# Block-sparse attention with a gated feed-forward, one core: other places for copies, turns, squares, tables and group entries

## The chip, the core and the metric

The kernel runs on one core of one Trainium2 chip. The core has a matrix engine (PE; PEld is its weight load), VectorE (DVE), ScalarE (ACT), GpSimd (POOL), a queue engine (SP), and 16 DMA engines. Each engine executes its own instructions strictly in the order in which the program issues them, and waits on semaphores for the others. The metric is the time of one execution in microseconds, the median of several runs.

## The reference, cut to what matters

```python
# q, k, v: (4 batches, 8 heads, 768, 64); blocks of 32, 24 blocks a sequence
scores = (q @ k.T) / sqrt(64)
# a query block sees: itself and one block either side, blocks 0 and 23, and three sampled blocks;
# query blocks 0 and 23 see everything
attn = softmax(where(mask, scores, -1e9)) @ v
x = attn with the heads side by side            # (3072, 512)
xn = x / sqrt(mean(x*x) + 1e-6) * rms_g
out = (silu(xn @ w_gate) * (xn @ w_val)) @ w_out   # 512 -> 1536 -> 512, float32
```

## The kernel before

**Passage.** Batch 0 is computed densely with a mask, in three groups of 256 queries (`groups`), each looping over the 8 heads `h`. A head makes two score parts (L527, three matmuls each, exponentials on ACT, L530) and, one head later, the product with the values (`late_pv` -> `pv`, L536, then reciprocal and scaling into `stage` on DVE, L545 and L546). At four points of each head `position()` takes pieces of the feed-forward of the group before out of the list `fill`; `small_work(gi, h)` follows each of these points. During the last group (`gi == 2`) the keys and queries of batch 1 are turned (`turn_first` -> `turn`, six PE transposes into a bank `tqk`, L455, and one copy into `KT1` or `QN1`, L457), the indices are worked out (`indices`, L385 to L410), the table of values is written (`table`, L446), and the first sparse chunk's keys (`gather_k`, `sampled_k`: L471, L476, L485), values (`gather_v`, L512) and queries (`gather_q`: `Qd`, L500) are collected. The queries' copies wait in `first_queries`, ScalarE's copies of sampled keys in `first_keys`. `after_pv` puts the squares of the group (`part_squares`, L570) into `later` or runs them; `dense_power` on POOL (L577), `dense_scale` (L585) and `dense_turn` (L596, L600) follow.

**Banks.** A matmul writes into one of eight PSUM banks. In the passage `bank()` gives out three of them in turn (the ring), for gate, value, down, turned and other tiles; one more ("ot", from `ps_o`) holds the product with the values and some turns; four are the score buffers. After the passage `bank()` goes round all eight. So a bank is free for the third (later the eighth) request after its own, once its reader is done.

**Feed-forward.** A group's pieces are, for twelve blocks `f` in turn, `gate(f)` (L732; tanh on ACT, L736) and `val(f)` (L743; on DVE `u`, L747, frees the gate's bank, and `hps`, L751, frees the value's bank), then four `down` parts (L761) a chunk, each of which needs three of the `hps`. `enter` sets the rate: the pieces in the list over the positions up to the next entry.

**Sparse steps.** Batches 1 to 3 are 18 chunks of 128 queries, six a batch, in six groups of 2, 3, 4, 4, 3, 2 chunks. Step `i` has ten positions `n`; `do(n, f)` lists a job at position `n`, and after a position's jobs one `position()` follows. Step `i` multiplies chunk `i-1` with its values (`values`, L644, at 0 and 1), normalises it (`normalise`, L669 and L670, at 1 and 2), squares it on ACT at 4, takes the power on POOL at 5 (L681, L682), scales and turns it at 7 (`x_turned`: `xs` on DVE, L694, and a transposing DMA of SP's queue into `xg`, L696); it makes chunk `i`'s scores from position 1 on (L620), and collects chunk `i+1` (`nx`): the window of the keys on DVE (`gk[0]`, 1536 columns), for the first two chunks of a batch also the edge keys (`gk[1:]`), sampled keys on POOL and ACT, the queries (`gq`, four copies, eight for the chunk of edge blocks), and the values by POOL's indirect DMA (two for `nx` at 1 and 2, two for `nx+1` at 6 and 7). One batch's keys, queries and table are made ready during the batch before.

Of the kernel before, what the change touches and what calls it, by code (L numbers as in the profile page):

```python
# [18 lines left out]
def kernel(  # L19
# [425 lines left out]
    def table(b):  # L445
        nc.gpsimd.dma_start(out=vtab[b][0:NT, :].rearrange("(p c) x -> p (c x)", c=HC),  # L446
                            in_=Vs[b % 2].rearrange("p c h x -> p (c h x)"))
# [60 lines left out]
    def gather_v(i, js=range(QB)):  # L508
        b, qbs = chunks[i]
        for j in js:  # L510
            if qbs[j] not in (0, NB - 1):
                nc.gpsimd.indirect_dma_start(  # L512
                    vgs[i % 3][:, j, :], None, vtab[b][:],
                    bass.IndirectOffsetOnAxis(ap=vidx[:, qbs[j]:qbs[j] + 1], axis=0))
# [52 lines left out]
    def part_squares(e, it, lo, hi):  # L567
        junk = work.tile([P, DM], BF16, name="junk", tag="junk", bufs=1)
        part = e["stage"][:, it, lo:hi]
        nc.vector.tensor_tensor_reduce(  # L570
            out=junk[:, 0:hi - lo], in0=part, in1=part, scale=1.0,
            scalar=(e["ssq"][:, it:it + 1] if lo else DM * 1e-6),
            op0=ALU.mult, op1=ALU.add, accum_out=e["ssq"][:, it:it + 1])
# [229 lines left out]
    NPD = 4 * H  # L803

    def after_pv(e, h):
        if h == H - 3:
            later.append(lambda: part_squares(e, 1, 0, (H - 2) * D))
        if h == H - 2:
            later.append(lambda: part_squares(e, 0, 0, (H - 1) * D))
        if h == H - 1:  # L810
            for it in range(2):
                part_squares(e, it, (H - 2 if it else H - 1) * D, H * D)
            dense_power(e)

    def late_pv():
# [24 lines left out]
    def indices(n):  # L840
        for _ in range(n):
            if index:
                index.pop(0)()
# [55 lines left out]
    def small_work(gi, h):  # L899
        if gi == 1 and h > 3 or gi == 2 and h < 4:  # L900
            next_address()
        if first_keys:
            first_keys.pop(0)()

    def turn_first(gi, h):
        if gi == 1 and h in (0, 2, 4):
            transpose_qk(h // 2 + 1, 1, 1, HC, h == 0, (dve, dve))
        if gi == 2:
            for pr, which, copy, spare in {
                    1: ((0, 0, act, False), (0, 1, dve, True)),  # L910
                    2: ((1, 0, act, True), (1, 1, dve, True)), 3: ((2, 0, act, True),),
                    4: ((2, 1, dve, True), (3, 0, act, True)), 5: ((3, 1, dve, True),)}.get(h, ()):
                turn(1, pr, which, copy, spare)
            if h == 5:
                first_queries.extend(gather_q(0, dve))
# [82 lines left out]
    for gi, grp in enumerate(groups):  # L998
        if gi == 0:
            continue  # L1000
        cur = begin(grp)
        for h in range(H):
            ex = ex_tile()
            thin = gi == 1 and h < TX
            dense_scores(grp, h, 0, ex)
            if h == 1 and ending is not None:
                dense_scale(ending, 1)
            if h == TX and ending is not None:
                dense_turn(ending, 0)
                if gi == 1:  # L1010
                    dense_turn(ending, 1)
                    enter_dense(ending, NPD + 4)
                    ending = None
            if thin and h > 0:
                keep_busy(1, 512)
            position()
            small_work(gi, h)
            if gi == 1 and h == 0:
                late_pv()
                last = late_pv()  # L1020
            dense_scores(grp, h, 1, ex)
            side_work(gi, h)
            position()
            small_work(gi, h)
            if thin:
                keep_busy(1, 512)
            if gi > 1 or h > 0:
                last = late_pv()
            if gi == 2:
                indices(5)  # L1030
            for _ in range(2 if first_queries else 0):
                first_queries.pop(0)()
            if last is not None:
                ending = last
            position()
            small_work(gi, h)
            position()
            small_work(gi, h)
            while later:
                later.pop(0)()  # L1040
            if h == TX and ending is not None:
                dense_turn(ending, 1)
                enter_dense(ending, NPD - 4 * TX - 4 + 10)
                ending = None
            turn_first(gi, h)
            if h == 0 and ending is not None:
                dense_scale(ending, 0)
            waiting.append((cur, h, ex))
# [8 lines left out]
    NPOS = 10  # L1057
    entry = {}
    for g, m in enumerate(sgroups[:-1]):
        entry[(min(m[-1] + 2, NCH), 3)] = g  # L1060

    def distance(i, n):

# [9 lines left out]
    for i in range(NCH + 1):  # L1073
        jobs = {}

        def do(n, f):
            jobs.setdefault(n, []).append(f)

        b, s = divmod(i, PB)
        b += 1  # L1080
        nx = i + 1 if i + 1 < NCH else None
        if i == 0:
            do(0, late_pv)
            do(3, lambda: dense_scale(cur, 0))
            do(3, lambda: dense_scale(cur, 1))
            do(5, lambda: dense_turn(cur, 0))
            do(6, lambda: dense_turn(cur, 1))
            do(6, lambda: enter_dense(cur, distance(0, 6)))
            do(4, lambda: nc.vector.memset(Qd[1], 0.0))
            do(3, lambda: load_kq(2, 3))  # L1090
            do(7, lambda: gather_v(1, (2, 3)))
        else:
            do(0, lambda: values(i - 1, 0))
            do(1, lambda: normalise(i - 1, 0))
            do(1, lambda: values(i - 1, 1))
            do(2, lambda: normalise(i - 1, 1))
            do(4, lambda: squares(i - 1))
            do(5, lambda: rms_power(i - 1))
            do(8 if i - 1 in sgroups[-1] else 7, lambda: x_turned(i - 1))
        if i < NCH:  # L1100
            n = bursts(i)
            for part in range(n):
                do(1 + part, lambda part=part: scores(i, part))
        if b + 1 < B and s <= NP:
            if s < NP:
                do(9 if s == 0 else 0, lambda: cast_v(b + 1, s, act))
            if s > 0:
                do(6, lambda: turn(b + 1, s - 1, 0, act, True))
                do(9, lambda: turn(b + 1, s - 1, 1, act, True))
            if s == 0 and b == 1:  # L1110
                do(8, lambda: nc.vector.memset(Vs[0][:, :, :, D:VW], 1.0))
            if s == NP - 1:
                do(2, lambda: table(b + 1))
        if nx is not None:
            at = 6 if nx == 1 else 0
            gk, gq = list(gather_k(nx, dve)), list(gather_q(nx, dve))
            do(at, gk[0])
            for m, x in enumerate(gk[1:]):
                do(min(at + 1, 8) + m, x)
            for m, x in enumerate(gq):  # L1120
                do(at + (3 if at == 0 else 1) + m * 4 // len(gq) * (at == 0) + m // 2 * (at > 0), x)
            kact, kpool = sampled_k(nx, "act"), sampled_k(nx, "pool")
            for x in kpool:
                do(at, x)
            for m, x in enumerate(kact):
                do(at + (m + 1) * (NPOS - 1 - at) // len(kact), x)
            if nx > 1:
                do(1, lambda: gather_v(nx, (2,)))
                do(2, lambda: gather_v(nx, (3,)))
            if nx + 1 < NCH:  # L1130
                do(6, lambda: gather_v(nx + 1, (0,)))
                do(7, lambda: gather_v(nx + 1, (1,)))
        for m in range(min(6, len(by_need)) if i < 2 else 0):
            do(m, next_address)

        bl, sl = divmod(i + 2, PB)
        if 0 < bl and bl + 2 < B and sl < NP:
            do(9, lambda: load_kq(bl + 2, sl))
        bv, sv = divmod(i + 3, PB)
        if 0 < bv and bv + 2 < B and sv < NP:  # L1140
            do(7, lambda: load_v(bv + 2, sv))
        for n in range(NPOS):
            if (i, n) in entry:
                g = entry[(i, n)]
                enter(ffn_pieces(xgs[g], sizes[g], chunk_store(sgroups[g])), distance(i, n))
            for x in jobs.get(n, ()):
                x()
            position()
# [35 lines left out]
```

## Time and profile before

| | |
|---|---|
| median of 3 runs (range) | 296.19 us (296.06 to 297.59) |
| the profiled execution: its own time, span | 295.37 us, 293.6 us |
| granted clock of PE | 0.998 |
| PE busy | 277.5 us (95%) |
| DVE, ACT, POOL busy | 216.4, 197.6, 151.5 us |
| passage with batch 1's turns (the last dense group) | from 44 to 77 us |
| first, second, third feed-forward group of sparse chunks enter at | 105.9, 133.8, 168.5 us |

A line of the timeline reads: start and duration in us, engine, line, operation, out<-in, count, and in brackets how long the engine had stood idle just before and what ended that. Seven instructions merged into one line are written x7. Since matmuls overlap, the next matmul may start before the one in the line has ended.

### The profile page before, as it was taken

The numbers are of one execution on the slowest core, as the hardware profiler recorded it, in microseconds if no ns is written. First come the engines' busy times: TensorE is split into PE (matmuls) and PEld (weight loads), VectorE is DVE, ScalarE is ACT, GpSimd is POOL, SyncE is SP. The second block draws the span as 40 slices with busy tenths as digits, with TensorE's granted clock in tenths as the row PEclk, the third lists the DMA queues.
The fourth block names the chain that finished last, engine by engine and source line by source line (L and its number), as shares of the span: only waits on it lengthen the run. The fifth ranks groups of instructions, "written<-read, shape, count | busy, mean of one in ns | idle before, by whom it ended". The sixth has DMA issues, their size and how long they took to land.

```text
span 293.6 us, 9868 instructions
## 1 busy us (share of the span) xinstructions
PE 277.5 (95%) x3863; PEld 184.2 (63%) x3863; DVE 216.4 (74%) x596; ACT 197.6 (67%) x466; POOL 151.5 (52%) x247
## 2 busy tenths in 40 slices
PE   8898999897899999699989999999999999899995
PEld 6686885776577678565655555545545456555783
DVE  7888887778889949966998479885399931784480
ACT  4996785677488888669999777577747484522431
POOL 9948135669587653885888463637641710001000
PEclk9999999999999999999999999999999999999999
DMA  7999999997986488997997933517740523000102
GB/s 134 297 215 201 208 206 281 301 262 216 175 238 165 131 279 154 163 239 237 227 190 198 311 107 99 145 44 201 232 120 2 138 78 82 36 2 36 74 1 71
DMA packets 38514, 47.70 MB, mean 162 GB/s; under 512 B 12272, under 2 KB 30468, under 8 KB 38468
## 3 DMA queue, kind: packets, MB, share of 16 engines
q0 software_dynamic: 21184, 32.60, 50.8%
q1 hardware_dynamic: 17220, 14.45, 16.8%
q8 instruction: 30, 0.49, 0.6%
q14 instruction: 16, 0.13, 0.1%
q10 hardware_dynamic: 64, 0.03, 0.1%
HBM read 46.45 MB, written 8.83 MB: 188 GB/s over the span
## 4 chain that ended last, share of the span: by engine, by line
PE 73%; DVE 13%; DMA 6%; issue 3%; POOL 2%; ACT 2%; DVEq 0%; ACTq 0%; POOLq 0%
PE gp L732 18%; PE vp L743 18%; PE yp L761 17%; PE st L620 6%; PE op L644 5%; DMA gain<-in_moe_rms_g_dram 4%; PE st L527 3%; DVE u L747 3%; DVE hps L751 2%; PE op L536 2%; DMA xg<-xs 2%; PE tqk L455 1%; PE unread L228 1%; POOL vg L512 1%; DVE junk L570 1%
## 5 line engine op out<-in xcount | busy, mean ns | idle before, releaser
L732 PE MATMUL gp<-xg,wg 128*128 128x256 bf16 (+2 forms) x432 | 80.7, 308 | 2.6 <-DVE stage L670 1.5
L743 PE MATMUL vp<-xg,wv 128*128 128x256 bf16 (+2 forms) x432 | 80.3, 308 | 3.0 <-DVE u L747 1.6
L512 POOL DMA_INDIRECT vg<-vtab,vidx x66 | 66.7, 1010 | 18.1 <-issue 12.2
L736 ACT ACTIVATE th<-gp 128x256 bf16<-128x256 f32 (+2 forms) x108 | 50.0, 466 | 33.6 <-PE gp L732 27.8
L761 PE MATMUL yp<-wo,hps 128*128 128x512 bf16 (+1 forms) x300 | 71.6, 371 | 0.0
L747 DVE SCALAR_TENSOR_TENSOR u<-th,gp 128x256 bf16<-128x256 bf16 (+2 forms) x108 | 54.6, 505 | 22.2 <-ACT th L736 20.7
L628 ACT ACTIVATE ex<-st 128x512 bf16<-128x512 f32 x84 | 50.5, 601 | 22.4 <-PE st L620 18.7
L751 DVE TENSOR_TENSOR hps<-u,vp 128x256 bf16<-128x256 bf16 (+2 forms) x108 | 55.1, 510 | 11.9 <-PE vp L743 0.8
L732 PEld LDWEIGHTS <-wg 128*128 128x128 bf16 x432 | 39.7, 98 | 21.1 <-issue 2.1
L743 PEld LDWEIGHTS <-wv 128*128 128x128 bf16 x432 | 38.7, 98 | 19.2 <-issue 2.8
L681 POOL TENSOR_TENSOR ssq<-ssq,eps 128x1 f32<-128x1 f32 x18 | 3.5, 194 | 72.3 <-ACT junk L677 68.3
L761 PEld LDWEIGHTS <-hps 128*128 128x128 bf16 x300 | 26.1, 98 | 20.5
L530 ACT ACTIVATE ex<-st 128x768 bf16<-128x768 f32 x42 | 33.3, 812 | 6.4 <-PE st L527 6.2
L766 ACT ACTIVATE yo<-yp 128x512 f32<-128x512 f32 (+1 forms) x25 | 14.5, 581 | 18.7 <-PE yp L761 18.6
L527 PE MATMUL st<-wide_q,wide_k 88*128 88x256 bf16 x144 | 23.2, 272 | 1.5 <-DVE wide_q L345 1.1
L644 PEld LDWEIGHTS <-ex 128*32 128x32 bf16 x1344 | 14.0, 96 | 13.1 <-issue 12.8
L694 DVE SCALAR_TENSOR_TENSOR xs<-stage,rstd,gain 128x512 bf16<-128x512 bf16 x16 | 12.4, 777 | 6.8 <-POOL rstd L682 6.6
L644 PE MATMUL op<-vg,ex 128*32 128x66 bf16 x1056 | 17.1, 195 | 0.1
L527 PEld LDWEIGHTS <-wide_k 88*128 88x128 bf16 x144 | 13.0, 98 | 5.5 <-DVE wide_q L345 2.4
L620 PEld LDWEIGHTS <-kg 128*128 128x128 bf16 x272 | 12.3, 98 | 6.2 <-issue 1.3
L620 PE MATMUL st<-Qd,kg 128*128 128x64 bf16 x272 | 14.8, 193 | 1.5 <-DVE stage L546 1.0
L670 DVE TENSOR_TENSOR stage<-op,rz 128x256 bf16<-128x256 f32 x36 | 15.3, 424 | 1.2
(149 smaller groups left out, 382.3 us busy)
## 6 DMA issues: line engine op xcount, KB each, us to landing
out_dram<-yo SPq DMA_DIRECT2D x20, 256.0 KB, 2.0
vraw<-in_v_dram SPq DMA_DIRECT2D x12, 384.0 KB, 7.5
kbf<-in_k_dram POOLq DMA_DIRECT2D x15, 192.0 KB
vtab<-Vs POOLq DMA_DIRECT2D x3, 792.0 KB
qbf<-in_q_dram POOLq DMA_DIRECT2D x12, 192.0 KB
vraw<-in_v_dram POOLq DMA_DIRECT2D x4, 384.0 KB
wg<-in_moe_w_gate_dram POOLq DMA_DIRECT2D x4, 384.0 KB
wv<-in_moe_w_val_dram POOLq DMA_DIRECT2D x4, 384.0 KB
```

Source lines behind the costliest of these rows:

```text
L512: nc.gpsimd.indirect_dma_start(vgs[i % 3][:, j, :], None, vtab[b][:], bass.IndirectOffsetOnAxis(ap=vidx[:, qbs[j]:qbs[j] + 1], axis=0))
L527: nc.tensor.matmul(out=at[:, e], lhsT=KT0[0:KR, h, jt * P:(jt + 1) * P], rhs=QT0[0:KR, h, c0 * P:(c0 + 2) * P], start=True, stop=True)
L530: nc.scalar.activation(out=ex[:, 3 * part:3 * (part + 1), :], in_=at[:, 0:3], func=AF.Exp, scale=SCALE)
L620: nc.tensor.matmul(out=st[:, at:at + UN], lhsT=lhsT, rhs=Qd[i % 2][:, h, :, :, j * HB:(j + 1) * HB].rearrange("p a w s -> p (a w) s"), sta ...
L628: nc.scalar.activation(out=ex.rearrange("p (u s w) -> p u s w", s=HB, w=2), in_=st.rearrange("p (u w s) -> p u s w", s=HB, w=2), func=AF.E ...
L644: nc.tensor.matmul(out=op[j * BLK:(j + 1) * BLK, at:at + VW], lhsT=lhsT, rhs=rhs, start=(n == 0), stop=(n == of - 1))
L732: nc.tensor.matmul(out=gp[:, 0:tg], lhsT=wg[:, c, f * P:(f + 1) * P], rhs=xg[:, c, 0:tg], start=(c == 0), stop=(c == KD - 1))
L736: nc.scalar.activation(out=th[:, 0:tg], in_=gp[:, 0:tg], func=AF.Tanh, scale=0.5)
L743: nc.tensor.matmul(out=vp[:, 0:tg], lhsT=wv[:, c, f * P:(f + 1) * P], rhs=xg[:, c, 0:tg], start=(c == 0), stop=(c == KD - 1))
L747: nc.vector.scalar_tensor_tensor(out=u[:, 0:tg], in0=th[:, 0:tg], scalar=1.0, in1=gp[:, 0:tg], op0=ALU.add, op1=ALU.mult)
L751: nc.vector.tensor_tensor(out=hps[f][:, 0:tg], in0=u[:, 0:tg], in1=vp[:, 0:tg], op=ALU.mult)
L761: nc.tensor.matmul(out=yp, lhsT=hps[f][:, tt * P:(tt + 1) * P], rhs=wo[:, f, lo:hi], start=(f == 0), stop=(f == NF - 1))
```

## The change

1. Passage, squares: for the last dense group the squares of the first 128 queries are taken in one piece of 512 columns after the last head, in place of 448 columns one head earlier and 64 at the end. The middle group keeps its cuts.
2. Passage, turns: pair 0's keys go into a ring bank rather than "ot"; pair 1's queries are turned a head later (3 rather than 2), into "ot"; pair 3's keys (head 4) go into "ot"; pair 3's queries (head 5) are copied by ACT rather than DVE.
3. Passage, small work: six index instructions a head rather than five; the first chunk's four query copies go one to each `small_work`, so all four come in head 6, rather than two each in heads 6 and 7 behind the product with the values.
4. Sparse steps: for every `nx` but 1, `gk[0]` goes from position 0 to 4 (behind both normalisations), `gk[1:]` from 1 and 2 to 6, the query copies from 3, 4, 5, 6 to 3 and 5 (half each).
5. The table of batches 2 and 3 goes from position 2 of one step to position 0 of the next, behind the last cast; the first two value gathers of a new batch's first chunk go from positions 6 and 7 to 8 and 9.
6. A feed-forward group enters at position 4 rather than 3.

```diff
     def after_pv(e, h):
-        if h == H - 3:
-            later.append(lambda: part_squares(e, 1, 0, (H - 2) * D))
-        if h == H - 2:
-            later.append(lambda: part_squares(e, 0, 0, (H - 1) * D))
+        cut = [H - 1, H - 2] if e["grp"] == groups[1] else [0, H - 2]
+        for it in range(2):
+            if cut[it] and h == cut[it] - 1:
+                later.append(lambda it=it: part_squares(e, it, 0, cut[it] * D))
         if h == H - 1:
             for it in range(2):
-                part_squares(e, it, (H - 2 if it else H - 1) * D, H * D)
+                part_squares(e, it, cut[it] * D, H * D)
...
-        if first_keys:
-            first_keys.pop(0)()
+        for x in (first_keys, first_queries):
+            if x:
+                x.pop(0)()
...
-                    1: ((0, 0, act, False), (0, 1, dve, True)),
-                    2: ((1, 0, act, True), (1, 1, dve, True)), 3: ((2, 0, act, True),),
-                    4: ((2, 1, dve, True), (3, 0, act, True)), 5: ((3, 1, dve, True),)}.get(h, ()):
+                    1: ((0, 0, act, True), (0, 1, dve, True)),
+                    2: ((1, 0, act, True),), 3: ((2, 0, act, True), (1, 1, dve, False)),
+                    4: ((2, 1, dve, True), (3, 0, act, False)), 5: ((3, 1, act, True),)}.get(h, ()):
...
-                indices(5)
-            for _ in range(2 if first_queries else 0):
-                first_queries.pop(0)()
+                indices(6)
...
-        entry[(min(m[-1] + 2, NCH), 3)] = g
+        entry[(min(m[-1] + 2, NCH), 4)] = g
...
-            if s == NP - 1:
-                do(2, lambda: table(b + 1))
+            if s == NP:
+                do(0, lambda: table(b + 1))
...
-            do(at, gk[0])
-            for m, x in enumerate(gk[1:]):
-                do(min(at + 1, 8) + m, x)
-            for m, x in enumerate(gq):
-                do(at + (3 if at == 0 else 1) + m * 4 // len(gq) * (at == 0) + m // 2 * (at > 0), x)
+            if at == 0:
+                for m, x in enumerate(gq):
+                    do(3 + m * 2 // len(gq) * 2, x)
+                do(4, gk[0])
+                for x in gk[1:]:
+                    do(6, x)
+            else:
...
-                do(6, lambda: gather_v(nx + 1, (0,)))
-                do(7, lambda: gather_v(nx + 1, (1,)))
+                at = 6 if (nx + 1) % PB else 8
+                do(at, lambda: gather_v(nx + 1, (0,)))
+                do(at + 1, lambda: gather_v(nx + 1, (1,)))
```

More of the change, by code (lines that the diff above doesn't have):

```diff
@@ L1116 @@
             gk, gq = list(gather_k(nx, dve)), list(gather_q(nx, dve))
-            do(at, gk[0])
-            for m, x in enumerate(gk[1:]):
-                do(min(at + 1, 8) + m, x)
-            for m, x in enumerate(gq):
-                do(at + (3 if at == 0 else 1) + m * 4 // len(gq) * (at == 0) + m // 2 * (at > 0), x)
+            if at == 0:
[5 more added lines that the diff above has]
+            else:
+                do(at, gk[0])
+                for m, x in enumerate(gk[1:]):
+                    do(at + 1 + m, x)
+                for m, x in enumerate(gq):
+                    do(at + 1 + m // 2, x)
             kact, kpool = sampled_k(nx, "act"), sampled_k(nx, "pool")
```

## The prediction

> **What bounds the kernel now.** I read the page first: PE is busy for 95% of the span, so a change that leaves PE's work alone can only win back its idle time, 16 us, or add to it. Then the list of what PE waited for: nearly every entry is a DVE instruction, so the question is what stands ahead of those instructions on DVE. Then a table by stretch, to see where PE is idle, and for those places the timelines of PE, DVE, ACT and POOL.
>
> The page:
>
> ```profile
> span 293.6 us, 9868 instructions
> PE 277.5 (95%) x3863; PEld 184.2 (63%) x3863; DVE 216.4 (74%) x596; ACT 197.6 (67%) x466; POOL 151.5 (52%) x247
> ```
>
> PE's waits (total, times, longest): u and the scaled stage release PE late, and only once does a DMA.
>
> ```profile
> PE vp L743 <- DVE u L747: 1.6, 2, 1.1
> PE gp L732 <- DVE stage L670: 1.5, 2, 0.8
> PE st L620 <- DVE stage L546: 1.0, 1, 1.0
> PE vp L743 <- DVE stage L670: 1.0, 2, 0.8
> PE gp L732 <- DMA xg<-xs: 0.5, 1, 0.5
> ```
>
> The stretches (PE, PEld, DVE, ACT, POOL busy): 2.79 us of PE's idle time lies in 64 to 77, the end of the passage, 0.48 in 85 to 102, 2.56 in 108 to 125. DVE is the fullest after PE in all three.
>
> ```profile
> 64.00:77.00 13.00, 10.21 (x125) 8.23 (x124) 11.70 (x39) 7.90 (x22) 9.29 (x15) 1.00 0.87 248
> 85.00:102.00 17.00, 16.52 (x278) 13.06 (x277) 15.38 (x43) 15.14 (x45) 12.06 (x22) 1.00 0.60 176
> 108.00:125.00 17.00, 14.44 (x296) 12.13 (x294) 15.35 (x47) 13.75 (x40) 10.93 (x19) 1.00 0.92 182
> ```
>
> PE's timeline where it waits; the bracket is the idle time just before:
>
> ```profile
> 57.52 0.60 PE L732 MATMUL gp<-xg,wg 128*128 128x256 bf16 x4 [0.63 <-DVE u L747]
> 61.06 0.50 PE L455 MATMUL tqk<-ident,kbf 128*128 128x128 bf16 x6 [0.30 <-DVE u L747]
> ...
> 122.47 0.61 PE L743 MATMUL vp<-xg,wv 128*128 128x256 bf16 x4 [0.79 <-DVE stage L670]
> 124.08 0.61 PE L732 MATMUL gp<-xg,wg 128*128 128x256 bf16 x4 [0.69 <-DVE stage L670]
> 150.97 0.82 PE L732 MATMUL gp<-xg,wg 128*128 128x384 bf16 x4 [0.82 <-DVE stage L670]
> 168.53 1.02 PE L732 MATMUL gp<-xg,wg 128*128 128x512 bf16 x4 [0.48 <-DMA xg<-xs]
> ```
>
> DVE and POOL, the instructions that the change moves, and one that is stretched:
>
> ```profile
> 51.63 0.81 DVE L405 TENSOR_TENSOR good<-good,tmp 48x24 f32<-48x24 f32 x1
> 65.67 0.96 DVE L457 COPY QN<-tqk 128x768 bf16<-128x768 bf16 x1
> 74.33 0.62 DVE L570 CUSTOM_DVE_ANT_0 junk<-stage 128x448 bf16<-128x448 bf16 x1
> 84.54 0.42 DVE L747 SCALAR_TENSOR_TENSOR u<-th,gp 128x256 bf16<-128x256 bf16 x1 [0.84 <-ACT th L736]
> 121.15 0.72 DVE L471 COPY kg<-wide_k 128x1536 bf16<-128x1536 bf16 x1
> 148.69 0.56 DVE L471 COPY wide_q<-wide_k 128x1536 bf16<-128x1536 bf16 x1
> ```
>
> ```profile
> 51.57 0.83 POOL L438 CAST Vs<-vraw 128x768 bf16<-128x768 f32 x1 [0.86 <-DMA vraw<-in_v_dram]
> 65.56 1.47 POOL L471 COPY kg<-KT 128x1536 bf16<-128x1536 bf16 x1
> ```
>
> **The change part by part.** The profiled execution took 295.37 us by its own time (span 293.6, 1.77 around it); the median shown is 0.82 above that. I sum against 295.37 and add 0.82 at the end.
>
> *Passage, copy and squares.* From 63.4 to 75.4 DVE is idle for 0.20 in all, and PE waits for it at 69.41 (0.56), 73.09 (1.08) and 75.51 (1.02): what leaves DVE here brings PE forward one for one. The last queries' copy at 65.67 holds DVE until 66.55, 0.88; the 448-column square until the next instruction at 74.88, 0.55. Together -1.43. The copy goes to ACT, 0.81 by its copies of that size; ACT is idle there for 0.39 (before 66.00), 0.35 (before 70.38) and 0.59 (before 72.05), which cover it. Without that cover, tanh and so u come 0.8 late, and the query copies behind the copy too.
>
> *Passage, banks and indices.* At 57.52 PE waits 0.63 for a u that stands behind the two index instructions of 56.27 to 57.04; with six a head they are done earlier. At 61.06 it waits 0.30 for a u that frees the ring bank for keys that will go to "ot". Both go: -0.93. Nothing is won before 55, since DVE waits there for the gain's DMA (54.66, idle 0.32). There is one ring request fewer behind them, and the first scoring step of chunk 0 takes a ring bank, free 0.23 before the one it waits for at 75.51: -0.2. The square of 512 columns after the last stage costs 0.40 more than 64 columns there (0.69, estimated from 0.35, 0.55 and 0.62 for 128, 384 and 448 columns, against 0.28). It delays rstd and `xs`, whose end would come at 77.3, while PE turns it at 78.8: nothing. With that cover gone, +0.40.
>
> *Passage, query copies.* All four now come in head 6. The first would reach DVE at about 65.7, while POOL's 1.47 us copy runs (65.56 to 67.03, fixed by the table's landing and the gathers in front). The trace has one such meeting: the index instruction at 51.63 took 0.81 rather than the 0.19 of its kind, and ended as POOL's cast did (52.40). If the copy is held in the same way it stands till 67.03, +1.2. The other end: the two pairs of query copies took 0.81 and 0.90 beside POOL's next copies, so 0.50 and 0.59 for the held one against 0.29, at most 0.3. Bounds 0 to +1.4; I take +1.2, by the nearest case, a small instruction beside a long one of POOL. The Trainium skill ("SBUF — State Buffer", section "SBUF: two separate sides") says that VectorE and GpSimd share a port pair as an exclusive lock, taken for a whole instruction by VectorE's two-port modes or two SBUF inputs, and that the other "fully blocks". The trace agrees at 51.63; by that rule the sum below stays, and by the pairs' own rows it would be 0.9 lower.
>
> The passage: -1.43 - 0.93 - 0.2 + 1.2 = -1.4 (-2.6 to -0.2).
>
> *First stretch, 84.5 to 102.* DVE has no idle time in it. At step 1 the key window, today at 83.03, in front of the 0.84 of idle at 84.54, moves behind the normalisations: +0.47 (a 0.56 copy's pitch, 148.69 to 149.16). Entering a position later spreads 36 pieces over one position fewer, and the last value piece falls behind `xs` (91.34 to 92.00): +0.66. Against it PE has some 0.45 more of its own work before the down part at 101.00, whose `hps` ends at 101.0 with nothing to spare. Net +0.65 (0 to +1.05).
>
> *Second stretch, 107 to 125.* The normalisations release the banks for which PE waits at 113.58 (0.22), 122.47 (0.79) and 124.08 (0.69); u for which it waits at 119.91 (0.85): 2.55 in all. The key window before the first of the late normalisations goes (121.15 to 121.78, 0.63), and the edge keys before the second (0.20); two query copies (0.59 together) come earlier, into idle time; one u and `hps`, 0.86, come behind the second normalisation rather than before. That is up to 2.3, but the next down part can start no more than 1.05 earlier than now for its own `hps` (126.78 against 127.83), and some of the rest comes back later: I take -1.2 (-0.3 to -1.6).
>
> *Third stretch, 145 to 152.* The key window ahead of the normalisation holds DVE from 148.69 to 149.16, 0.47 of the wait of 0.82 at 150.97: -0.5 (0 to -0.8, the whole wait).
>
> *Entry one position later.* The 0.48 at 168.53 is a wait for the transposed `xg` (DMA 5.0 after `xs`). A position is over 1 us: -0.5 (0 to -0.5). The earlier groups' entries have no such wait.
>
> *Tables and gathers.* POOL issues the table in 0.60 and nothing of SP's queue moves. From issue to the first gather it took 5.9 (54.76 to 60.70). For batch 2 the table would be issued behind rstd at about 109, and the gather comes at about 116.9, 7.9 later: 2.0 of cover, so 0. With that cover gone, POOL waits for the table, and the next rstd, `xs` and `xg` by as much. The query copies as half each at two positions rather than a quarter at four change no total on DVE: 0.
>
> Sum: -1.4 + 0.65 - 1.2 - 0.5 - 0.5 = -2.95, so 292.4 own time; with 0.82, **293.2 us**.
>
> **The rivals.** *A, no hold and a free first stretch.* The query copy isn't held (-1.2) and the 0.84 of DVE's idle before 84.54 with PE's extra work covers the first stretch (-0.65): 293.2 - 1.85 = 291.3. For it: the copies' own rows, 0.50 and 0.59; against it: the row at 51.63.
>
> *C, the stretches give it back.* What PE doesn't wait for in the second and third stretch it waits for at the next down part, since DVE has the same work in them. Left are -1.4, +0.65 and -0.5, -1.25: 294.9. For it: DVE busy 15.4 of 17 in both; against it: the waits name the normalisation.
>
> *D, slower: a down part waits in each stretch.* The copies now fall between the last u and `hps` of a group and the down part that needs them, where today they stand ahead. In the first stretch that costs its upper bound, 1.05 (0.47 and 0.66, against little more PE work), in the others the 0.63 and 0.59 of window and query copies (1.22) and 0.47 with 0.66 (1.1): +3.4, and no gain there. With -1.4 and -0.5 it is +1.5: 297.7. It decides once the three sum to more than 1.9. For it: no slack at 101.00; against it: 1.05 at 127.8, and over 1.2 after 152.
>
> *The change doesn't do what it says:* every move is of an instruction with a row, so only the late entries and banks could miss, which is C.
>
> **How the numbers follow.** Forecast 0.38, A 0.28, C 0.17, D 0.17. Alone, the forecast's bounds give 292.2 to 294.4. The range reaches to A with a further 1.1 (the full 1.6 in the second stretch, 0.3 in the third and the first's rest), 290.2, and towards D, to 297.0. A measurement of this kernel tells about 0.5% from no change, 294.7 to 297.7: forecast and A are faster (0.66), C is within it (0.17), D slower (0.17).
>
> **What would show it.** In the changed kernel: no QN copy and no 448-column square on DVE between 64 and 76, and PE's idle time there down from 2.8 to about 1.5; the first query copy lasting over 1 us and ending with POOL's window copy (A: 0.5 or less); no wait of PE near 57.5 and 61; the down part of the first stretch waiting some 0.6 for `hps` (D: over 1); no waits for stage L670 of 0.7 and more between 120 and 125, nor at 151; none for xg at 168. Waits for vidx or table on POOL would be what I hold covered. The prediction falls if a down part waits over 1 us in two stretches, or if ACT, with the extra copy, holds up a tanh in the passage.

## The result and the profile after

The changed kernel takes 295.03 us (median of 20 runs) against 296.07 of the kernel before beside it: ratio 0.996, 95% interval 0.9941 to 0.9979, some 1.0 us less. A second set of runs (e1 below) gave 0.9983 (0.9956 to 1.001). Ratios leave out the runs in a slower state, which the medians count, so the two can differ a little. The forecast was 3.0 us less. The gain is clear of the noise in the first set but not in the second, and it is within the 0.5% that the prediction counts as no change. It is about where rival C stood (294.9), though not for C's reason.

The profiled execution of the changed kernel took 296.42 us by its own time (span 294.6), 1.4 above its median, so a second trace of the same kernel (experiment e1, own time 295.65, span 293.9) is read beside it everywhere below.

The page of the changed kernel, busy time by engine:

```profile
span 294.6 us, 9864 instructions
PE 278.3 (94%) x3863; PEld 185.1 (63%) x3863; DVE 216.1 (73%) x593; ACT 199.2 (68%) x467; POOL 150.5 (51%) x247
```

What PE waited for in it (total, times, longest). The waits for the stages L546 and L670 have shrunk from 4.0 to 1.2, and two single waits of 1.7 at a gate have come:

```profile
PE vp L743 <- DVE u L747: 1.9, 3, 1.1
PE gp L732 <- DMA xg<-xs: 1.7, 1, 1.7
PE gp L732 <- ACT ex L628: 1.7, 1, 1.7
...
PE gp L732 <- DVE stage L670: 0.5, 2, 0.3
PE st L620 <- DVE stage L670: 0.5, 1, 0.5
```

The stretches of the changed kernel (window, its length, then PE, PEld, DVE, ACT, POOL busy):

```profile
64.00:77.00 13.00, 11.16 (x138) 8.81 (x136) 11.56 (x37) 8.96 (x23) 9.99 (x15) 1.00 0.89 258
85.00:102.00 17.00, 16.29 (x288) 12.33 (x289) 15.40 (x43) 15.49 (x44) 13.45 (x22) 1.00 0.60 167
108.00:125.00 17.00, 16.22 (x328) 12.98 (x326) 15.52 (x48) 15.09 (x44) 12.22 (x20) 1.00 0.93 178
125.00:135.00 10.00, 7.70 (x189) 4.64 (x186) 4.91 (x16) 5.84 (x16) 6.89 (x13) 1.00 1.25 259
```

PE's idle time fell from 2.79 to 1.84 in the passage's end and from 2.56 to 0.78 in the second stretch. It rose from 0 to 2.30 between 125 and 135, where the kernel before had PE busy for all of 10.00 us.

PE's timeline of the changed kernel, the waits that are left and the new ones:

```profile
69.60 0.60 PE L743 MATMUL vp<-xg,wv 128*128 128x256 bf16 x4 [1.07 <-DVE u L747]
117.59 0.60 PE L743 MATMUL vp<-xg,wv 128*128 128x256 bf16 x4 [0.51 <-DVE u L747]
134.35 0.81 PE L732 MATMUL gp<-xg,wg 128*128 128x384 bf16 x4 [1.66 <-ACT ex L628]
151.21 0.82 PE L732 MATMUL gp<-xg,wg 128*128 128x384 bf16 x4 [0.30 <-DVE stage L670]
169.62 1.02 PE L732 MATMUL gp<-xg,wg 128*128 128x512 bf16 x4 [1.73 <-DMA xg<-xs]
```

The two gates at 134.35 and 169.62 are the first of the second and third feed-forward group: the entries. The releaser printed at 134.35 is not the one. The instruction waits for the xg of its group's three chunks and for the reader of its bank. That reader was done at 127.1, and the exponential that is named (133.63 to 134.23) reads another bank. The last xg was issued at 127.12 and landed 7.1 later, at 134.3. In every trace of e1 to e8 with a wait at this gate, the gate starts 0.09 after that landing, while the instruction that is named differs:

```profile
xg<-xs SPq DMA_TRANSPOSE x1, 7.1
```

So the places can be compared by adding up the brackets (0.15 us and more) of PE's timeline:

| PE waits, us | before | after | e1 (the same kernel) |
|---|---|---|---|
| passage, 44 to 77 | 4.21 | 1.95 | 3.33 |
| first stretch, to 106 | 0.48 | 0.71 | 0.66 |
| second stretch, to 128 | 2.55 | 0.74 | 0.74 |
| entry near 134 | 0 | 2.31 (0.65 of it at 129.27, no releaser) | 1.19 |
| third stretch, 138 to 160 | 0.82 | 0.48 | 0.24 |
| entry near 169 | 0.48 | 1.73 | 1.07 |
| turn of the last groups, 256 | 0.80 | 1.01 | 1.01 |

These leave out smaller gaps and what differs by chance before 44 us (2.9, 3.1 and 3.7 of waits there, in code that the change doesn't touch), so their sums (9.3, 8.9, 8.2) follow the spans only roughly.

### The profile page after: what moved, and what is told of

It reads as the page before. It is cut to its first block, busy times and chain, and to the rows that moved or that the text cites. A ratio compares the mean times of both kernels' runs of the same rounds, so it can differ in the third digit from the quotient of the medians.

```text
span 294.6 us, 9864 instructions
## 1 busy us (share of the span) xinstructions
PE 278.3 (94%) x3863; PEld 185.1 (63%) x3863; DVE 216.1 (73%) x593; ACT 199.2 (68%) x467; POOL 150.5 (51%) x247
## 4 chain that ended last, share of the span: by engine, by line
PE 66%; DVE 18%; POOL 6%; issue 5%; DMA 3%; ACT 1%; DVEq 0%; ACTq 0%; POOLq 0%
PE gp L732 17%; PE vp L743 16%; PE yp L761 16%; PE st L620 5%; DVE hps L751 3%; PE op L644 3%; DVE u L747 3%; PE st L527 3%; POOL vg L512 3%; DMA xg<-xs 3%; PE tqk L455 2%; PE op L536 2%; PE unread L228 1%; DVE junk L570 1%; DVE stage L670 1%
## 5 line engine op out<-in xcount | busy, mean ns | idle before, releaser
L512 POOL DMA_INDIRECT vg<-vtab,vidx x66 | 66.1, 1001 | 18.0 <-issue 12.6
L743 PEld LDWEIGHTS <-wv 128*128 128x128 bf16 x432 | 39.5, 98 | 19.9 <-issue 3.3
L669 DVE RECIPROCAL rz<-op 128x4 f32<-128x4 f32 x36 | 6.4, 177 | 13.7 <-PE op L644 13.5
L670 DVE TENSOR_TENSOR stage<-op,rz 128x256 bf16<-128x256 f32 x36 | 15.3, 424 | 1.2
L620 PE MATMUL st<-wide_q 128*128 128x64 bf16 x256 | 15.3, 193 | 0.1
```

Of the source, the lines that this page charges most:

```text
L512: nc.gpsimd.indirect_dma_start(vgs[i % 3][:, j, :], None, vtab[b][:], bass.IndirectOffsetOnAxis(ap=vidx[:, qbs[j]:qbs[j] + 1], axis=0))
L620: nc.tensor.matmul(out=st[:, at:at + UN], lhsT=lhsT, rhs=Qd[i % 2][:, h, :, :, j * HB:(j + 1) * HB].rearrange("p a w s -> p (a w) s"), sta ...
L743: nc.tensor.matmul(out=vp[:, 0:tg], lhsT=wv[:, c, f * P:(f + 1) * P], rhs=xg[:, c, 0:tg], start=(c == 0), stop=(c == KD - 1))
```

## The experiments

Each was timed in five rounds beside the kernel before. Most intervals of e1 to e8 are about 0.27% to either side, 0.8 us, so a difference of under a microsecond between two variants is read from the traces and not from the medians.

**First question: is the xg late at the entries because of DMAs beside it, or because of one execution, or because of DVE?** In the changed kernel POOL issues the kbf and qbf of batch 3 at 126.66 and 127.42, about when SP issues the xg (127.12), and the table of batch 3 at 161.06, just ahead of the xg at 161.98. The kernel before issues the same pair of loads, but just behind its xg, and its gate at 133.78 doesn't wait. SP, POOL and PE of the kernel before, then SP and POOL of the changed kernel:

```profile
128.21 1.20 SPq L696 DMA_TRANSPOSE xg<-xs  x1
128.23 0.80 POOL L126 DMA_DIRECT2D kbf<-in_k_dram  x1
133.78 0.81 PE L732 MATMUL gp<-xg,wg 128*128 128x384 bf16 x4
```

```profile
127.12 1.29 SPq L696 DMA_TRANSPOSE xg<-xs  x1
126.66 0.80 POOL L126 DMA_DIRECT2D kbf<-in_k_dram  x1
```

e1, the changed kernel unedited.

> The changed kernel once more, as the measure for the other runs and for a second trace. Theory (collision): the passage and the three stretches gain what was forecast, and the third and fourth feed-forward entry give it back, because the transposing DMA of the last xs of a group runs beside DMAs that POOL issues next to it: ratio to the kernel before 0.996 again, and PE waits at the first gate near 134 and near 169 for more than 1.5 us in sum. Rival (one execution): the two waits of 1.66 and 1.73 belong to the one profiled execution; then they are absent here, and the time is below 0.993. Rival (late copies): the waits are there, but because xs itself comes late behind the copies on DVE; the DMA takes 4 to 5 us as before.

Measured: 295.77 against 296.41, ratio 0.9983 (0.9956 to 1.001). Both entry waits are there, 1.19 and 1.07. They belong to the kernel and not to one execution. DVE's copies are not the main part: PE comes to the gate near 134 5.57 after the issue of its xg in the kernel before, and 5.57 and 4.80 after it in the two traces of the changed kernel, so at most 0.8 of e1's wait can come from a late xs. But the passage's wait near 70 is larger than in the first trace. PE and DVE of e1, the first query copy and whom it delays:

```profile
71.02 0.60 PE L743 MATMUL vp<-xg,wv 128*128 128x256 bf16 x4 [1.87 <-DVE u L747]
134.55 0.81 PE L732 MATMUL gp<-xg,wg 128*128 128x384 bf16 x4 [1.19 <-ACT junk L677]
168.87 1.02 PE L732 MATMUL gp<-xg,wg 128*128 128x512 bf16 x4 [1.07 <-DMA xg<-xs]
```

```profile
67.19 2.71 DVE L500 COPY Qd<-QN 64x512 bf16<-64x512 bf16 x1
69.95 0.29 DVE L500 COPY Qd<-QN 64x512 bf16<-64x512 bf16 x1
```

e2, tables and gathers back:

```diff
-            if s == NP:
-                do(0, lambda: table(b + 1))
+            if s == NP - 1:
+                do(2, lambda: table(b + 1))
...
-                at = 6 if (nx + 1) % PB else 8
-                do(at, lambda: gather_v(nx + 1, (0,)))
-                do(at + 1, lambda: gather_v(nx + 1, (1,)))
+                do(6, lambda: gather_v(nx + 1, (0,)))
+                do(7, lambda: gather_v(nx + 1, (1,)))
```

> The changed kernel with the tables of batches 2 and 3 and the first two gathers of a new batch's first chunk back at their old positions. Collision: the table of batch 3 is issued five positions ahead of the xs near 162 rather than three behind it, so the transposing DMA takes about 5 us rather than 7.4, and PE's wait at the entry near 169 falls from 1.7 to under 0.6: 1.0 to 1.5 us below the changed kernel, ratio to before 0.991 to 0.993. Late copies: the table has nothing to do with it, 0.996, the wait at 169 stays over 1.

Measured: 295.00, ratio 0.9955 (0.9927 to 0.9982). The xg near 162 lands in 5.9 rather than 6.7 and 7.4, and the wait at 169 is 0.39. By this run alone the table is the cause; e3 and e4 contradict it.

e3, one pair of loads six positions later:

```diff
-        if 0 < bl and bl + 2 < B and sl < NP:
+        if 0 < bl and bl + 2 < B and sl < NP and i != 5:
             do(9, lambda: load_kq(bl + 2, sl))
+        if i == 6:
+            do(5, lambda: load_kq(3, 1))
```

> The changed kernel with one pair of loads (kbf and qbf of batch 3, pair 1) issued six positions later, behind the feed-forward entry near 134, where it was issued beside the last xs of that group. Collision: the transposing DMA takes 3 to 4 us rather than 7.2, and PE's wait of 1.66 near 134 goes: 1.0 to 1.7 us below the changed kernel, ratio to before 0.990 to 0.993. Late copies: no effect, 0.996, wait of 1 or more at 134.

Measured: 295.53, ratio 0.9973 (0.9941 to 1.0005). The transposing DMA near 128 tells its landing in sixteen updates of a semaphore. In e3 fifteen of them came by 3.2 us after the issue, against 4.4 to 7.1 in the two traces with the loads beside it; but the sixteenth came at 5.8, and the gate waits for all, so PE still waited 1.04. The wait at 169 fell to 0.40 here too, with the table at its new place.

e4, both edits.

> The two together. Collision: both waits go, 2.0 to 3.0 us below the changed kernel, ratio to before 0.986 to 0.990, which is about the forecast of 293.2. Late copies: 0.996. One execution: all four kernels the same within 0.2%.

Measured: 296.08, ratio 0.998 (0.9954 to 1.0006), none of the 2 to 3 us. The xg near 129 lands in 4.8 (fifteen parts in 4.0), and the gate at 133.96 starts without a wait. But the next entry takes it: the xg near 163 lands in 6.5, with the table back at its old place.

```profile
133.96 0.81 PE L732 MATMUL gp<-xg,wg 128*128 128x384 bf16 x4
```

```profile
169.77 1.02 PE L732 MATMUL gp<-xg,wg 128*128 128x512 bf16 x4 [1.59 <-DMA xg<-xs]
```

What follows: with the loads ahead of it most of the xg near 128 lands later. Fifteen parts came in 3.2 and 4.0 without them, and in 5.0 to 7.1 with them in the traces of after, e1 and e2; the last part, for which the gate waits, came at 5.8 and 4.8 against 5.9 to 7.1. The order may be what counts. In the kernel before and in e7 (below) the first load is issued 0.01 to 0.02 behind the xg, and no gate waits (landed in 4.85 in e7, in at most 5.6 in the kernel before). In the changed kernel, e1, e5, e6 and e8 it is issued 0.46 to 0.48 ahead of the xg, in e2 1.69, and the xg landed in 5.9 to 7.1. No run changes that order alone. The table is not shown to matter. And a wait taken away at one entry can be there again at the next.

**Second question: what eats the passage's gain?**

e5, the query copies a head later:

```diff
-                first_queries.extend(gather_q(0, dve))
+                first_queries.extend([lambda: None] * 4 + list(gather_q(0, dve)))
```

> The changed kernel with the first sparse chunk's four query copies one head later (head 7, one at each small_work), when POOL's three key copies are over. In five traces of the changed kernel and its variants the first of these copies took 1.91, 2.71, 2.63, 2.84 and 3.22 us and ended each time within 0.6 of the end of POOL's run of key copies. Theory (port): it is held for the whole run of POOL's copies, and this eats the passage's gain. Then each copy takes 0.3 to 0.6 here, PE's wait of 1.2 to 2.6 near 70 goes, and the time is 1.3 to 2.3 us below the changed kernel: ratio to before 0.990 to 0.993. Rival (order): the copies cost because they stand ahead of u on DVE, wherever they are; then PE's wait only moves one head on, and the ratio stays at 0.996 to 0.998.

e6, POOL's key copies ahead of its gathers:

```diff
-                gather_v(0)
                 for x in [*gather_k(0, pool), *sampled_k(0, "pool")]:
                     x()
+                gather_v(0)
```

> The changed kernel with POOL's key copies for the first sparse chunk ahead of its four value gathers rather than behind them; DVE's order is that of the changed kernel. Port: POOL's copies are then over (about 62 to 66) when the first query copy comes, which takes 0.3, or it meets their last part and takes under 1.5; 1.0 to 2.3 us below the changed kernel, ratio 0.990 to 0.994. Order: nothing changes on DVE, ratio 0.996 to 0.998.

Measured: e5 295.61, ratio 0.9977 (0.9954 to 1.0001); e6 295.75, ratio 0.996 (0.9931 to 0.9989). The hold is as the port theory has it; the times are where its rival had them (0.996 to 0.998). POOL of the changed kernel, and DVE of the changed kernel, of e5 and of e6, in this order:

```profile
65.67 1.47 POOL L471 COPY kg<-KT 128x1536 bf16<-128x1536 bf16 x1
67.09 1.15 POOL L476 COPY kg<-KT 128x512 bf16<-128x512 bf16 x2
68.19 1.25 POOL L485 COPY kg<-KT 128x128 bf16 x4
```

```profile
66.57 1.91 DVE L500 COPY Qd<-QN 64x512 bf16<-64x512 bf16 x1
68.53 0.29 DVE L500 COPY Qd<-QN 64x512 bf16<-64x512 bf16 x1
```

```profile
70.77 0.28 DVE L500 COPY Qd<-QN 64x512 bf16<-64x512 bf16 x1
```

```profile
67.41 0.55 DVE L500 COPY Qd<-QN 64x512 bf16<-64x512 bf16 x1
```

The same copy takes 1.91 to 3.22 (five traces) beside POOL's run of copies, 0.28 behind it and 0.55 with the run moved away, at the same place in DVE's order. It ends with the run of large copies (68.48 against 68.24 here), not with the one of them that it met. PE's wait of 1.07 to 2.39 near 70 is gone in both. Some of it is found a little later, as the order rival had it: e5 waits 0.59 at 72.25 and 0.73 at 74.37, the second for a query copy, and e6 0.57 at 71.80. The passage's waits sum to 2.52 (e5) and 1.60 (e6) against 3.33 in e1.

And yet no more time is won than with the copy held. At the entries of e5, and at the first entry of e6:

```profile
133.91 0.81 PE L732 MATMUL gp<-xg,wg 128*128 128x384 bf16 x4 [1.84 <-ACT wide_q L485]
169.27 1.02 PE L732 MATMUL gp<-xg,wg 128*128 128x512 bf16 x4 [2.14 <-DMA xg<-xs]
```

```profile
134.44 0.81 PE L732 MATMUL gp<-xg,wg 128*128 128x384 bf16 x4 [2.43 <-ACT wide_q L485]
```

In e5 PE came to the entry at 132.07 and in e1 at 133.36, so 1.29 of gain had arrived there; the gate itself started at 133.91 and 134.55, only 0.64 apart. In e6 PE came at 132.01 and the gate started at 134.44: of 1.35 only 0.11 was left. Each time the gate started about 0.1 after its xg had landed. The xg had been issued 1.2 and 1.3 earlier than in e1 (127.32 and 127.27 against 128.56), but took 6.5 and 7.1 to land, against 5.9 in e1. Why it took longer these runs don't show. e6 has no wait at 169.

e7 and e8, the two halves of the change alone: e7 is the kernel before with items 1 to 3 of the change, e8 the kernel before with items 4 to 6, each the diff shown with the change.

> The kernel before with the parts on the passage alone (squares, turns, small work). Port: the passage gains 1.43 + 0.93 + 0.2 = 2.6 and loses 1.6 to 2.9 to the held copy: 0 to -1.0 us, ratio 0.997 to 1.0. Order: the same. The forecast was -1.4, ratio 0.995.

> The kernel before with the parts on the sparse steps alone (copies behind the normalisation, later tables and group entries). By the traces of the changed kernel the second and third stretch gain 1.8 and 0.7, the first loses 0.6 to 0.9, and the entries near 134 and 169 wait 1.0 to 1.7 for the transposed xg: -2.5 + 0.7 + 2 = 0 to +0.5 us, ratio 0.998 to 1.002. The forecast was -1.55, ratio 0.995.

Measured: e7 295.68, ratio 0.9979 (0.9958 to 1.0001), 0.6 less. Its copy was held for 3.17, and the passage's waits are 3.06 against 4.21. It also waits 2.63 at the entry near 169, where the xg took 7.3 to land rather than the 5.0 of the kernel before. The sparse steps, table included, are there those of the kernel before, so the longer transfer does not need items 4 to 6. e8: 297.95, ratio 1.0061 (1.0033 to 1.0089), 1.8 more, beyond either expectation. In e8's trace the second stretch has 1.18 of waits against 2.55, but the entry near 134 waits 1.61 (xg issued 130.15, landed after 6.5), and a down part in the first stretch waits for its `hps`, as rival D had it for that place:

```profile
104.47 0.39 PE L761 MATMUL yp<-wo,hps 128*128 128x512 bf16 x1 [0.84 <-DVE hps L751]
136.77 0.81 PE L732 MATMUL gp<-xg,wg 128*128 128x384 bf16 x4 [1.61 <-issue]
```

The halves add to +1.2 and the whole is -0.5 to -1.0. The wait at the down part is only there without the passage's half. Why that is so these runs don't show.

**What the runs show beside the question: PE's granted clock.** In three of these traces it is 0.5 for a stretch of 3.4 us, from 70.8 in e2, 70.5 in e7 and 135.3 in e6. Each begins within 0.9 of the end of a wait of PE of 1.8 or more (at 70.07, 70.58 and 134.44); waits as long in e1, e3, e4 and e5 have none behind them. Of the executions in the ratios, the mean granted clock is under 0.998 in 2 of 68 of the kernel before beside e1 to e8, and in 7 of 30 of the changed kernel (2 of 18 in the first set, 5 of 12 in e1). In e1 those five take 296.4 on average, the other seven 295.5. So the changed kernel loses some 0.4 us there. Long waits of PE may be what brings the lower clock about; no edit tested that.

**Third question: would a later entry keep the gain?** These ten runs fell on three other chips (e9 to e12, e13 to e16, e17 and e18), where the kernel before took 311 to 314 us. In each trace PE's granted clock is 0.5 for one to four stretches of 3.4 us, one of which begins between 87 and 92, and PE pauses without a releaser for 9.8 to 14.2 in all (none in e1, counting from 0.15). So PE lost several microseconds ahead of the entries in question.

e9, entry at 6; e10, entry at 3; e11, item 4 of the change undone; e12, entry at 6 together with the edits of e3 and e6:

```diff
-        entry[(min(m[-1] + 2, NCH), 4)] = g
+        entry[(min(m[-1] + 2, NCH), 6)] = g
```

> The changed kernel with its feed-forward groups entering at position 6 rather than 4. Theory (entry): whatever PE gains before 134 it waits for at the first gate of the entering group, because the group's last xg lands 5.9 to 7.8 us after its issue (PE's waits there 1.2 to 2.4 in six traces). Two positions are over 2 us: the waits near 134 and 169 fall below 0.3 each, and if nothing else takes their place the time falls by 1.0 to 2.5, ratio to before 0.988 to 0.993. Rival (spread): a group's 36 pieces over fewer positions crowd DVE in front of the down parts, PE waits there instead, and the ratio is 0.997 or more.

> The changed kernel with its groups entering at position 3, as before the change. Entry: PE comes to the first gate a position (0.7 to 1.0) earlier, the xg lands no earlier, so the waits near 134 and 169 grow by 0.7 to 1.0 in sum, and the time is 0.3 to 1.0 above the changed kernel, ratio 0.998 to 1.001. Spread: the first group's pieces have a position more, PE's work is better spread, 0.3 to 0.7 below the changed kernel, ratio 0.993 to 0.996.

> The changed kernel with the key and query copies of the sparse steps back at their old positions (tables, gathers, entry and passage as changed). The forecast gave these copies -1.2 and -0.5 in the second and third stretch and +0.5 in the first. Entry: the waits of 0.7 to 0.8 for the scaled stage return near 122, 124 and 151, and the wait at 134 shrinks by about as much: within 0.5 of the changed kernel, ratio 0.995 to 0.999. If the copies' gain is real and kept: 1.0 to 1.5 above the changed kernel, ratio 1.0 to 1.003.

> The changed kernel with entry at position 6, POOL's first key copies ahead of the value gathers, and the one pair of loads behind the entry near 134. Entry and port together: no query copy over 0.6, no wait near 71 over 0.6, none at the two entries over 0.5: 2.5 to 4.0 us below the kernel before, ratio 0.986 to 0.992. If one of the two is wrong: 0.993 to 0.997.

Measured, ratios to the kernel before on the same chip: e9 1.012 (1.0054 to 1.0187), e10 1.0153 (1.0086 to 1.0219), e11 1.0105 (1.0061 to 1.0149), e12 1.0207 (1.013 to 1.0284). No run of the changed kernel stands beside these four. In e11 the second group's first gate still waits 1.16, so undoing item 4 does not take that wait away.

e13, the changed kernel on the second of these chips; e14, e9 again; e15, the edits of e3 and e6; e16, e12 again; e17, e9 a third time; e18, e15 again.

> The changed kernel again, reference for the three runs beside it: ratio to the kernel before 0.995 to 0.999 where the granted clock is 1.0, the first query copy held for 1.9 to 3.2, waits of over 1 at the entry near 134.

> The changed kernel with entry at position 6. Entry theory: no wait over 0.3 near 134 and 169, 1.0 to 2.5 us below the changed kernel beside it. Spread: PE waits for hps at down parts or for u instead, within 0.5 of the changed kernel or above it.

> The changed kernel with POOL's first key copies ahead of the value gathers (query copy not held) and the one pair of loads behind the entry near 134, entry still at 4. Port and collision together: first query copy under 0.6, the xg near 128 lands 3.2 to 4.8 after issue for most of its 16 parts, wait at 134 under 0.7; 1.5 to 2.5 below the changed kernel. If a gain ahead of 134 is lost at the entry whatever loads run beside it: within 0.5.

> The changed kernel with POOL's first key copies ahead of the gathers, the pair of loads later, and entry at 6. Entry and port: 2.5 to 4.0 below the kernel before, ratio 0.986 to 0.992. Spread: 0.994 to 1.0.

> The changed kernel with entry at position 6. At a granted clock of 1.0, entry theory: no wait of PE over 0.3 at the first gates near 134 and 169, ratio to before 0.988 to 0.994. Spread: PE waits in front of down parts or for u by as much instead, 0.996 to 1.004. At a granted clock under 0.95 around 90 us: 1.01 as in the two runs before, and the question stays open.

> The changed kernel with POOL's first key copies ahead of the value gathers and the one pair of loads behind the entry near 134. At a granted clock of 1.0, port and collision together: first query copy 0.3 to 0.6, PE's wait near 134 under 0.7, ratio to before 0.988 to 0.993. If the gain ahead of 134 is lost at the next entry instead: 0.995 to 0.998 with a wait of 2 or more near 169. At a granted clock under 0.95 around 90 us: 1.007 as in the run before.

Measured: e13 0.9968 (0.9929 to 1.0006), e14 1.0108 (1.0068 to 1.0147), e15 1.0071 (1.0029 to 1.0113), e16 1.0202 (1.0145 to 1.026), e17 1.0103 (1.005 to 1.0156), e18 1.0116 (1.0057 to 1.0175). The changed kernel is 0.3% below the kernel before on its chip, with an interval that includes 1, and the three edits beside it are 1.0% to 2.3% slower than it. e13's first query copy took 0.53, not the 1.9 to 3.2 expected: in the traces with POOL's order as in the changed kernel (e9, e10, e11, e13, e14, e17) PE's pauses and waits bring that copy to the end of POOL's large copies or behind it, and it takes 0.28 to 0.53. So on these chips there was no hold to remove.

The waits at the entries go as the entry theory says. With entry at 3 (e10) the first gates of the first three groups wait 0.74, 0.93 and 2.59; with entry at 4 (e13) the first two wait 1.05 and 1.09 and the third not; with entry at 6 (e9, e12, e14, e16, e17) no first gate waits for an xg. With entry at 4 and the loads later (e15, e18) the second group's gate doesn't wait, as in e4, and the first group's waits 1.34 and 1.83 (in e18 the third group's too, 1.13). The gates of e10 and then those of e13. Where the releaser is "issue", the last xg landed 0.1 before; the landing before 144.26 is not in the trace:

```profile
115.77 0.60 PE L732 MATMUL gp<-xg,wg 128*128 128x256 bf16 x4 [0.74 <-DMA xg<-xs]
144.26 0.81 PE L732 MATMUL gp<-xg,wg 128*128 128x384 bf16 x4 [0.93 <-PE st L620]
184.11 1.86 PE L732 MATMUL gp<-xg,wg 128*128 128x512 bf16 x4 [2.59 <-issue]
```

```profile
113.98 0.60 PE L732 MATMUL gp<-xg,wg 128*128 128x256 bf16 x4 [1.05 <-DMA xg<-xs]
141.77 0.81 PE L732 MATMUL gp<-xg,wg 128*128 128x384 bf16 x4 [1.09 <-issue]
```

But the time does not follow. The engines' lines of e13 (span 307.9) and then of e14 (span 312.7):

```profile
PE 283.0 (92%) x3863; PEld 187.0 (61%) x3863; DVE 214.6 (70%) x593; ACT 198.7 (65%) x467; POOL 150.2 (49%) x247
PE 286.9 (92%) x3863; PEld 188.4 (60%) x3863; DVE 215.3 (69%) x593; ACT 198.4 (63%) x467; POOL 150.8 (48%) x247
```

From e13 to e14 PE's waits with a releaser fall from 8.3 to 7.2. Its pauses without one rise from 12.6 to 14.2, and the same 3863 matmuls are busy for 286.9 rather than 283.0 (277.9 in e1). That is +4.4 of a span that is 4.8 longer (the medians differ by 3.2). So in these two traces entry at 6 loses its time not in a wait in another place, as the spread theory had it, but in pauses and slower matmuls. e14 has two stretches at a granted clock of 0.5 (from 89.2 and 119.9), e13 one (from 89.5); 3.4 us at half the clock cost some 1.7, an estimate from these two figures. The rest is open, and so is why the clock falls. What entry at 6 is worth at a granted clock of 1.0 stays open, and no version was found that beats the changed kernel.

## Why the prediction was right or wrong

Its terms, against the waits in the two traces of the changed kernel:

| step | forecast | after | e1 |
|---|---|---|---|
| passage | -1.4 | -2.26 | -0.88 |
| first stretch | +0.65 | +0.23 | +0.18 |
| second stretch | -1.2 | -1.81 | -1.81 |
| entry near 134 | 0 | +2.31 | +1.19 |
| third stretch | -0.5 | -0.34 | -0.58 |
| entry near 169 | -0.5 | +1.25 | +0.59 |
| turn at 256 | 0 | +0.21 | +0.21 |

**Copy, squares, indices: right; banks: right in one trace.** The last QN copy and the 448-column square are gone from DVE, the square of 512 columns took the 0.69 estimated, and the waits at 57.52 and 61.06 are gone. ACT's copy (0.80) made PE wait for no tanh. But near 60 a wait for another u came in e1, e5 and e6 (0.72, 0.77 and 0.66), which is most of the 0.93 forecast there.

**Query copies: the mechanism right, the term too small.** I took +1.2, a hold till the end of the one copy of POOL that it meets. It is held for the whole run of POOL's large copies, and cost 1.6 to 2.9 over its own 0.29. The rule that I weighed, the Trainium skill's ("SBUF — State Buffer", section "SBUF: two separate sides"), speaks of a lock held "for the whole instruction". The traces agree that the copy is blocked. They show it blocked till the end of three instructions of POOL, where I had reckoned with one. By these terms, 2.6 of gains against the hold, the passage is worth between 1.0 and nothing; the waits fell by 2.26 and 0.88. Rival A's "not held" is refuted for this order of POOL's work.

**The three stretches: right in sign, and the second larger than forecast.** No wait for L670 above 0.3 is left between 107 and 160. Rival C, which had the gain given back at the next down part, is refuted for its place: no down part waits in the changed kernel. Rival D's wait at a down part came only in e8.

**The entry: the step that failed.** I wrote -0.5 for 169 and, for the others, that they "have no such wait". That is true of the kernel before, but I took the time of the transfer as given and read no slack. At 133.78 the first gate came 5.57 after the issue of its xg, eight of whose sixteen updates the trace has, the last of them 4.4 after the issue: at most 1.2 of slack, while I let 1.95 of gain (-1.4, +0.65, -1.2) pass through. In the changed kernel the xg's issue moved with part of the gain, and PE came 5.57 and (in e1) 4.80 after it; but the xg landed 7.1 and 5.9 after it. In e2 to e6 and e8 PE came 4.4 to 5.0 after the issue, and the xg landed 4.8 to 7.1 after it. So what PE gained ahead of 134 ended as a wait there, whichever part of the change had won it (e5, e6). At 169 the later entry did what I had it for: PE came 5.9 after the issue in both traces, 4.9 in the kernel before. But the xg took 7.4 and 6.7 (5.9 to 7.8 in the variants) rather than 5.0. Why the transfers take longer is not settled. The next late thing was a transfer, and I had looked for it on DVE only.

**The granted clock: not in the sum.** The prediction has no term for it. In e1 five of twelve executions were below 0.998, which is worth some 0.4 us on average (296.4 against 295.5, shown by the runs, cause not tested).

**Tables and gathers: 0, not refuted.** POOL waits for no table in the traces of after. By e2 the table's new place costs up to 0.7 at 169 against e1, by e3, e4 and e6 nothing.

**The sum.** The steps up to 128 were forecast at -1.95 and measured at -3.8 and -2.5; the entries, forecast at -0.5, measured at +3.6 and +1.8. The time of 295.03 lay in the range, in the case that had been given 0.17 for another mechanism; that hit is luck. One statement on the numbers doesn't follow from the terms: their bounds, added up, give 290.7 to 296.7, not the 292.2 to 294.4 given for the forecast alone.

## What to carry to other kernels

Before a gain is carried to the end of the sum, follow it to the next place where the engine needs something that does not get earlier with it, a transfer above all, and read that place's slack: issue, landing, arrival. A wait that is 0 in the kernel before says only that the slack is not negative, and a transfer's time can change when what is issued beside it moves. A small SBUF-to-SBUF copy on DVE is cheap only where POOL isn't in a run of copies; its price is up to the length of that run.

## What the runs showed that was not expected

- A DVE copy of 0.29 was held for 1.91, 2.63, 2.71, 2.84, 3.17 and 3.22 us by back-to-back copies of POOL (1.47, then 1.15 for two), and let in between the small ones that follow (1.25 for four).
- One transposing DMA lands in sixteen parts that can be far apart: fifteen by 3.2 us after its issue and the last at 5.8 (e3), fifteen by 5.3 and the last at 6.5 (e5).
- On the chips of e9 to e18 PE pauses without a releaser. In e13 it does so for 0.4 to 0.5 us every 0.70 to 0.76, at a granted clock of 1.0 (86 to 89), just ahead of the stretch at 0.5 that begins at 89.5:

```profile
86.96 0.23 PE L644 MATMUL op<-vg,ex 128*32 128x66 bf16 x4 [0.37 <-issue]
87.66 0.19 PE L644 MATMUL op<-vg,ex 128*32 128x66 bf16 x1 [0.47 <-issue]
88.42 0.25 PE L620 MATMUL st<-wide_q 128*128 128x64 bf16 x3 [0.41 <-issue]
```
